# Weights converted in pieces of 1024 columns, and token blocks in another order, in a retention and two-MLP kernel

## The chip, the cores and the metric

The kernel runs on one core of one Trainium2 chip. Its time is the device time of one execution in microseconds; three runs of the kernel before took 897.42 to 898.11 us, with a median of 897.6 us.

## The reference

Attention with a decay in place of a softmax (retention), then two MLPs with the same shapes:

```python
scores = q @ k.T / sqrt(64)            # batch 4, heads 8, seq 576, head_dim 64
x = (scores * Dmat) @ v                # Dmat[i, j] = gamma_h ** (i - j) for i >= j, else 0
x = x.transpose(0, 2, 1, 3).reshape(2304, 512)
h = x @ moe_w_in                       # 512 x 2048
x = (h * sigmoid(h)) @ moe_w_out       # 2048 x 512
r = maximum(x @ moe2_w_in, 0)
out = (r * r) @ moe2_w_out             # 2304 x 512, float32
```

The weights come as float64, the rest as float32.

## The kernel before

**The products.** Each float32 operand is split into a high and a low part (`xh`, `xl`, `wh`, `wl`, `gh`, `gl`), and each product is three matmuls: high by high, high by low, low by high (`mm3`, L74). The 2304 tokens are cut into five blocks (`BLOCKS`), and `d_ff` into 16 columns of 128 (`f`). `seq` lists the steps (layer, block, f). A step runs `gemm1` (12 matmuls, 4 of 128 rows by 3) into the PSUM tile `ph`, and `gemm2` of the step two earlier (`LAG`) into `acc`. Between the two stands `gate`: the activation on ScalarE (L380 or L383), the product on VectorE (L381 or L384, `sg`), the copy `gh` on ScalarE (L388) and the rest `gl` on VectorE (L389). `later` and `flush` put these off by half a step each, so that on every engine they stand behind what was emitted before them. Engines run their queues in order.

**The weights.** All 64 wide weight tiles don't fit at once beside the rest: a layer's 16 `wh` and 16 `wl` tiles take the 32 buffers of pool `wp`, and each passes from layer 0 to layer 1 when its last matmul is done. The float64 words are turned into float32 by bit operations, in pieces of 512 columns (`w_in` and `w_out` of an `f` are one piece each): `load_w` fetches a raw piece on SyncE's queue, `conv_a` makes two ScalarE passes (L101, L102), `conv_b` a shift, an add and a sign operation on VectorE (L107 to L109), `conv_c` copies `wh` on ScalarE (L121), `conv_d` makes `wl` on VectorE (L125). Raw pieces have three buffers (`RAW`), and the load of a piece is issued when `conv_b` of the piece three before it is done. `conv_to` says how far the conversion has got: in the start-up by the table `ST_C`, in the first block of layer 0 two pieces a step, in the last block of layer 0 and the first of layer 1 nine eighths of a piece a step.

**The attention.** Eighteen units of 128 tokens, each a score product `P` (`scores`), a state of the past that GpSimd decays (`dS`, L290) and VectorE adds to (`S`, L284 and L286), a value product `Q` (`values`), and `whole`, which puts the two halves together and splits the result into `xh` and `xl`. The four units of the first block run ahead of the first step (the start-up); those of block j + 1 are spread over the steps of block j.

**Between the layers.** Layer 0 writes its result to DRAM (`x2`). `load_x2` fetches a block back on SyncE's queue into `xr`, and four copies on ScalarE (L442, `xh`) and four differences on VectorE (L443, `xl`) follow at once on their queues. It is called at step 8 of the last block of layer 0 and at step 4 of each block of layer 1.

Of the kernel before, what the change touches and what calls it, by code (L numbers as in the profile page):

```python
# [38 lines left out]
def kernel(  # L39
# [21 lines left out]
    xp = ctx.enter_context(tc.tile_pool(name="xp", bufs=2))  # L61
# [17 lines left out]
    order = sorted(range(2 * KF), key=lambda i: (i // 2 + i % 2 * LAG, i % 2))

    def w_at(n):

        layer, i = divmod(n, 2 * KF)
        return (layer, *divmod(order[i], 2))

    def load_w(n):
        layer, f, part = w_at(n)
        if n < W1_FIRST:
            r = wp.tile([128, 512], U64, tag="w", name="wr")
        else:  # L90
            r = rp.tile([128, 512], U64, tag="wr", name="wr")
        nc.sync.dma_start(out=r, in_=(w1, w2)[layer][f, part])  # L92
        raw_w[n] = r

    conv = {}

    def conv_a(n):
        r = raw_w.pop(n).bitcast(I32).rearrange("p (n t) -> p n t", t=2)
        lo, hi = r[:, :, 0], r[:, :, 1]
        t = rp.tile([128, 512], I32, tag="wt", name="t", bufs=3)  # L100
# [12 lines left out]
    def w_part(n):  # L113
        layer, f, part = w_at(n)
        if (layer, f) not in wt:
            wt[layer, f] = tuple(wp.tile([128, 1024], F32R, tag="w", name=nm) for nm in ("wh", "wl"))
        return (w[:, part * 512 : part * 512 + 512] for w in wt[layer, f])

    def conv_c(n):
        wh, _ = w_part(n)  # L120
        nc.scalar.copy(wh, conv[n][0].bitcast(F32))  # L121

    def conv_d(n):
        wh, wl = w_part(n)
        nc.vector.tensor_sub(wl, conv.pop(n)[0].bitcast(F32), wh)  # L125
# [12 lines left out]
    load_end = [2 * KF]  # L138
# [7 lines left out]
    def conv_to(layer, n):  # L146

        for i in range(conv_n[layer], min(n, 2 * KF + 2)):
            conv_n[layer] += 1
            for lag, stage in ((2, conv_c), (0, conv_a), (1, conv_b), (2, conv_d)):  # L150
                if 0 <= i - lag < 2 * KF:
                    stage(layer * 2 * KF + i - lag)
                    if stage is conv_b and n_loaded[0] < i - lag + layer * 2 * KF + RAW + 1:
                        load_next()
# [6 lines left out]
    x_t = {}  # L161
    block_of = []
# [7 lines left out]
    dS = [None]  # L170
# [73 lines left out]
    def scores(u, startup):  # L244
# [11 lines left out]
        rf = ap.tile([128, 2, 4, L], F32, tag="rf", name="rf", bufs=2)  # L256
# [8 lines left out]

        def first_state():
# [5 lines left out]
    def new_state(u, b, P):  # L272
# [9 lines left out]
        add = P[:, b, 256:512].rearrange("p (a d) -> p a d", a=4)  # L282
        if n == 0:
            nc.vector.tensor_copy(new, add)  # L284
        else:
            nc.vector.tensor_add(new, add, dS[0])  # L286
# [106 lines left out]
    def gemm2(layer, j, f):  # L393
# [6 lines left out]
        for t in range(nt):  # L400
# [10 lines left out]
            if f == KF - 1:  # L411
# [23 lines left out]
    def load_x2(j):  # L435
# [3 lines left out]
        xh = xp.tile([128, KD, NBMAX], F32R, tag="xh", name="xh")[:, :, 0:n]  # L439
        xl = xp.tile([128, KD, NBMAX], F32R, tag="xl", name="xl")[:, :, 0:n]  # L440
# [31 lines left out]
    while n_loaded[0] < W1_FIRST:  # L472
        load_next()
# [112 lines left out]
```

## Time and profile before

| | |
|---|---|
| median of three runs | 897.6 us (897.42 to 898.11) |
| profiled execution | 897.14 us |
| its span | 895.4 us |
| TensorE matmul busy | 862.8 us (96%) |
| VectorE busy | 427.6 us (48%) |
| ScalarE busy | 327.1 us (37%) |
| GpSimd busy | 72.8 us (8%) |

The span is the time from the first to the last instruction; the rest of the execution lies around it. PE is TensorE, PEld its weight loads, DVE VectorE, ACT ScalarE, POOL GpSimd, SPq and ACTq the instructions that issue DMAs on SyncE's and ScalarE's queues. A busy time is a share of the whole span, while the stages have different limits, so the rows below are by stretch. An arrow in brackets names what ended the idle time before an instruction.

### The profile page before, as it was taken

The numbers are of one execution on the slowest core, as the hardware profiler recorded it, in microseconds if no ns is written. First come the engines' busy times: TensorE is split into PE (matmuls) and PEld (weight loads), VectorE is DVE, ScalarE is ACT, GpSimd is POOL, SyncE is SP. The second block draws the span as 40 slices with busy tenths as digits, with TensorE's granted clock in tenths as the row PEclk, the third lists the DMA queues.
The fourth block names the chain that finished last, engine by engine and source line by source line (L and its number), as shares of the span: only waits on it lengthen the run. The fifth ranks groups of instructions, "written<-read, shape, count | busy, mean of one in ns | idle before, by whom it ended". The sixth has DMA issues, their size and how long they took to land.

```text
span 895.4 us, 14028 instructions
## 1 busy us (share of the span) xinstructions
PE 862.8 (96%) x5930; PEld 739.8 (83%) x5930; DVE 427.6 (48%) x722; ACT 327.1 (37%) x594; POOL 72.8 (8%) x105
## 2 busy tenths in 40 slices
PE   6698979999999999999999989999999999999998
PEld 5576758999999888888878878889999888888886
DVE  3899995333443333335767776632242233223222
ACT  3576663222222322225556555432232223222221
POOL 5210111111122021100000000000000000000000
PEclk8699999999999999999999999999999999999999
DMA  9445532111211213002343433020020020001001
GB/s 355 175 140 191 181 127 95 48 48 48 84 49 48 84 48 118 1 1 95 120 139 118 142 131 115 2 83 1 1 83 1 0 83 1 1 0 48 1 1 47
DMA packets 21662, 68.27 MB, mean 76 GB/s; under 512 B 2400, under 2 KB 4192, under 8 KB 21216
## 3 DMA queue, kind: packets, MB, share of 16 engines
q1 hardware_dynamic: 17280, 59.91, 19.5%
q10 hardware_dynamic: 4320, 7.47, 2.3%
q8 instruction: 46, 0.75, 0.3%
q14 instruction: 16, 0.13, 0.0%
HBM read 57.93 MB, written 9.44 MB: 75 GB/s over the span
## 4 chain that ended last, share of the span: by engine, by line
PE 82%; DVE 2%; DMA 1%; issue 0%; ACT 0%; SPq 0%; ACTq 0%
PE acc L74 40%; PE ph L74 39%; PE Q L301 2%; DMA xr<-x 1%; PE P L250 1%; PE P L255 1%; DVE xl L443 0%; DVE t L108 0%; DVE gl L389 0%; DVE t L109 0%; DVE t L107 0%; DVE wl L125 0%; PE Q L317 0%; ACT xh L442 0%; SPq L92 0%
## 5 line engine op out<-in xcount | busy, mean ns | idle before, releaser
L74 PE MATMUL ph<-xh,wh 128*128 128x512 f32 (+1 forms) x640 | 238.1, 372 | 5.6 <-ACT xh L335 5.6
L74 PE MATMUL ph<-xl,wh 128*128 128x512 f32 (+1 forms) x640 | 236.4, 369 | 0.0
L74 PE MATMUL ph<-xh,wl 128*128 128x512 f32 (+1 forms) x640 | 236.3, 369 | 0.0
L384 DVE SCALAR_TENSOR_TENSOR sg<-ph,sg 128x512 f32<-128x512 f32 (+1 forms) x80 | 51.0, 638 | 195.3 <-ACT sg L383 195.3
L74 PEld LDWEIGHTS ph<-xh,wh 128*128 128x128 f32 x640 | 120.8, 189 | 24.0 <-ACT xh L335 5.8
L74 PEld LDWEIGHTS ph<-xl,wh 128*128 128x128 f32 x640 | 120.7, 189 | 16.8 <-DVE xl L336 0.4
L74 PEld LDWEIGHTS ph<-xh,wl 128*128 128x128 f32 x640 | 120.7, 189 | 15.2
L74 PE MATMUL acc<-gl,wh 128*128 128x512 f32 (+1 forms) x320 | 120.2, 376 | 9.6 <-DVE gl L389 9.4
L389 DVE TENSOR_TENSOR gl<-sg,gh 128x512 fp32r<-128x512 f32 (+1 forms) x160 | 103.5, 647 | 52.9 <-ACT gh L388 52.6
L388 ACT CAST gh<-sg 128x512 fp32r<-128x512 f32 (+1 forms) x160 | 92.3, 577 | 91.2 <-DVE sg L384 51.5
L381 DVE TENSOR_TENSOR sg<-ph,sg 128x512 f32<-128x512 f32 (+1 forms) x80 | 50.9, 636 | 148.7 <-ACT sg L380 148.7
L74 PE MATMUL acc<-gh,wh 128*128 128x512 f32 (+1 forms) x320 | 120.5, 377 | 0.0
L383 ACT ACTIVATE sg<-ph 128x512 f32<-128x512 f32 (+1 forms) x80 | 44.5, 556 | 207.9 <-PE ph L74 207.5
L74 PE MATMUL acc<-gh,wl 128*128 128x512 f32 (+1 forms) x320 | 119.0, 372 | 0.0
L74 PE MATMUL acc<-wh,gl 128*128 128x512 f32 x288 | 112.8, 392 | 2.8 <-DVE gl L389 2.8
L74 PE MATMUL acc<-wl,gh 128*128 128x512 f32 x288 | 112.6, 391 | 0.0
L74 PE MATMUL acc<-wh,gh 128*128 128x512 f32 x288 | 112.0, 389 | 0.0
L380 ACT ACTIVATE sg<-ph 128x512 f32<-128x512 f32 (+1 forms) x80 | 44.3, 554 | 159.0 <-PE ph L74 159.0
L74 PEld LDWEIGHTS acc<-gl,wh 128*128 128x128 f32 x320 | 60.8, 190 | 21.3 <-DVE gl L389 13.9
L74 PEld LDWEIGHTS acc<-gh,wh 128*128 128x128 f32 x320 | 60.6, 189 | 8.7
L74 PEld LDWEIGHTS acc<-gh,wl 128*128 128x128 f32 x320 | 60.9, 190 | 7.4
L74 PEld LDWEIGHTS acc<-wh,gl 128*128 128x128 f32 x288 | 54.1, 188 | 14.6 <-DVE gl L389 3.2
(50 smaller groups left out, 738.0 us busy)
## 6 DMA issues: line engine op xcount, KB each, us to landing
wr<-w SPq DMA_DIRECT2D x64, 512.0 KB, 3.5
raw<-att SPq DMA_DIRECT2D x34, 512.0 KB, 5.3
x<-y ACTq DMA_DIRECT2D x12, 256.0 KB, 2.5
xr<-x SPq DMA_DIRECT2D x3, 1024.0 KB, 5.5
out<-y SPq DMA_DIRECT2D x10, 256.0 KB, 2.1
out<-y ACTq DMA_DIRECT2D x7, 256.0 KB, 2.3
x<-y ACTq DMA_DIRECT2D x8, 192.0 KB, 1.9
xr<-x SPq DMA_DIRECT2D x2, 768.0 KB, 5.3
```

Source lines behind the costliest of these rows:

```text
L74: mm(o, a, b, start=first and i == 0, stop=last and i == n - 1)
L250: mm(o, dims(u, a, e, b, 768), dims(u, a, e, b, 0), start=True, stop=True)
L255: mm(o, toks(u, a, e, b, 256), toks(u, a, e, b, 512), start=True, stop=True)
L301: mm(w, a, b, start=e not in started, stop=last)
L380: nc.scalar.activation(s, ph, ACTF.Sigmoid)
L381: nc.vector.tensor_mul(s, ph, s)
L383: nc.scalar.activation(s, ph, ACTF.Relu)
L384: nc.vector.scalar_tensor_tensor(s, ph, 0.0, s, op0=ALU.max, op1=ALU.mult)
L388: nc.scalar.copy(gh, s)
L389: later.append(lambda: nc.vector.tensor_sub(gl, s, gh))
```

## The change

`w_in` and `w_out` of an `f` become one piece of 1024 columns, except for the first three `f` of layer 0, which stay in two pieces of 512 (all three `w_in` first). Raw pieces have two buffers of twice the size. The three operations of `conv_b` are cut in two parts, and the parts of three neighbouring pieces are interleaved by half steps: `conv_to` counts half pieces. `ST_C` and `ST_F` say how many in the start-up and in the first steps, then two a step; for layer 1 it is 0.8 pieces a step in the last block of layer 0 and half a piece a step in layer 1. The blocks are 512, 384, 512, 384, 512 tokens, layer 1 takes them in the order 1, 0, 3, 2, 4, and the tiles of x have one buffer for even and one for odd blocks. The decayed state is written in place by GpSimd ahead of VectorE's sum, in the start-up one flush later.

```diff
-BLOCKS = [512, 384, 384, 512, 512]
+BLOCKS = [512, 384, 512, 384, 512]
-W1_FIRST, W1_AHEAD = 6, 5
+W1_FIRST = 3
-ST_C = (0, 0, 1, 2, 2, 3, 3, 4, 4)
-W2_LAG, W2_NUM, W2_DEN = 0, 9, 8
+ST_C = (0, 0, 2, 3, 4, 5, 5, 6, 7)
+ST_F = (7, 11, 15, 18)
+W2_LAG = 1
-RAW = 3
+RAW = 2
...
+    pieces = (
+        [(0, f, part, 1) for part in range(2) for f in range(W1_FIRST)]
+        + [(0, f, 0, 2) for f in range(W1_FIRST, KF)]
+        + [(1, f, 0, 2) for f in range(KF)]
+    )
...
+            r = rp.tile([128, 2, 512], U64, tag="wr", name="wr")
+        w = (w1, w2)[layer][f, part : part + m].rearrange("a p c -> p a c")
+        nc.sync.dma_start(out=r, in_=w)
...
+    def conv_raw(n):
+        lo, hi = words(n)
+        bits[n] = t = rp.tile([128, 1024], I32, tag="wt", name="t", bufs=2)[:, 0 : 512 * pieces[n][3]]
         nc.scalar.activation(t.bitcast(F32), hi.bitcast(F32), ACTF.Abs, scale=2.0**-112)
         nc.scalar.activation(lo, lo.bitcast(U32), ACTF.Copy, scale=2.0**-29)
+    def conv_add(n):
+        t = bits[n]
         nc.vector.tensor_scalar(t, t, 3, None, op0=ALU.logical_shift_left)
+        nc.vector.tensor_tensor(t, t, words(n)[0], op=ALU.add)
+    def conv_sign(n):
+        t, hi = bits[n], words(n)[1]
         nc.vector.scalar_tensor_tensor(
             t, hi, -(2**31), t, op0=ALU.bitwise_and, op1=ALU.bitwise_or
         )
+        raw_w.pop(n)
+        if n_loaded[0] <= n + RAW:
+            load_next()
...
     def conv_to(layer, n):
-        for i in range(conv_n[layer], min(n, 2 * KF + 2)):
+        last = n_pieces[layer]
+        for i in range(conv_n[layer], min(n, 2 * last + 3)):
             conv_n[layer] += 1
...
+            k, odd = divmod(i, 2)
+            todo = ((0, conv_raw), (1, conv_sign), (1, conv_wh)) if odd else ((1, conv_add), (2, conv_wl))
+            for lag, stage in todo:
+                if 0 <= k - lag < last:
+                    stage(layer * n_pieces[0] + k - lag)
...
+    def new_x(j):
+        return tuple(
+            xp.tile([128, KD, BLOCKS[j % 2]], F32R, tag=f"{nm}{j % 2}", name=nm) for nm in ("xh", "xl")
+        )
+    J2 = (1, 0, 3, 2, 4)
...
         def first_state():
             new_state(u, 0, P)
-            later.append(lambda: new_state(u, 1, P))
-        later.append(first_state)
+            decayed_state(u, 1)
+            later.append(second_state)
...
+        later.append((lambda: later.append(first_state)) if startup else first_state)
...
             if layer == 0 and j == 0:
-                conv_to(0, 2 * f + half + 1 + W1_AHEAD)
-            elif i > w2_base + W2_LAG:
-                conv_to(1, (2 * (i - w2_base - W2_LAG) + half - 1) * W2_NUM // (2 * W2_DEN))
+                n0, n1 = (ST_F[x] if x < len(ST_F) else ST_F[-1] + 2 * (x - len(ST_F) + 1) for x in (f, f + 1))
+                conv_to(0, n1 if half else (n0 + n1 + 1) // 2)
+            elif i >= w2_base + W2_LAG:
+                h = 2 * (i - w2_base - W2_LAG) + half + 1
+                conv_to(1, 4 * min(h, 2 * KF) // 5 + max(h - 2 * KF, 0) // 2)
...
             if layer == 0 and j == nb - 1 and f == KF - 8:
-                load_x2(0)
-            if layer == 1 and f == 4 and j + 1 < nb:
-                load_x2(j + 1)
+                load_x2(J2[0])
+            if layer == 1 and f == 4 and j != J2[-1]:
+                load_x2(J2[J2.index(j) + 1])
```

VectorE in the first block, from the gate product of step 1 (`sg`) to that of step 2, before (`t` is a piece under conversion, the number behind a name tells tiles apart; `wl_605` is that of step 3):

```order
L381 TENSOR_TENSOR sg_599<-ph_575,sg_599 128x512
L107 TENSOR_SCALAR t_589<-t_589 128x512
L108 ISA t_589<-wr_152,t_589 128x1024
L109 SCALAR_TENSOR_TENSOR t_589<-wr_152,t_589 128x512
L125 TENSOR_TENSOR wl_605<-t_567,wh_604 128x512
L107 TENSOR_SCALAR t_607<-t_607 128x512
L108 ISA t_607<-wr_154,t_607 128x1024
L109 SCALAR_TENSOR_TENSOR t_607<-wr_154,t_607 128x512
L125 TENSOR_TENSOR wl_542<-t_589,wh_541 128x512
L389 TENSOR_TENSOR gl_601<-sg_599,gh_600 128x512
L381 TENSOR_TENSOR sg_641<-ph_617,sg_641 128x512
```

The same stretch after the change (`wl_608` is that of step 3):

```order
L418 TENSOR_TENSOR sg_574<-ph_552,sg_574 128x512
L123 SCALAR_TENSOR_TENSOR t_565<-wr_140,t_565 128x512
L118 TENSOR_SCALAR t_579<-t_579 128x1024
L119 ISA t_579<-wr_150,t_579 128x2048
L136 TENSOR_TENSOR wl_533<-t_565,wh_532 128x512
L123 SCALAR_TENSOR_TENSOR t_579<-wr_150,t_579 128x1024
L118 TENSOR_SCALAR t_601<-t_601 128x1024
L119 ISA t_601<-wr_152,t_601 128x2048
L136 TENSOR_TENSOR wl_608<-t_579,wh_607 128x1024
L426 TENSOR_TENSOR gl_576<-sg_574,gh_575 128x512
L418 TENSOR_TENSOR sg_614<-ph_588,sg_614 128x512
```

Between the same two products there were two narrow pieces, and step 3's `wl` was the fourth operation behind the first product; now it is the eighth, with two wide shifts and adds and a wide sign ahead of it.

ScalarE in the first block, in the steps that follow, before (`wr` is a raw piece; L101 and L102 read it first):

```order
L102 ACTIVATE wr_686<-wr_686 128x512
L388 CAST gh_735<-sg_734 128x512
L121 CAST wh_604<-t_720 128x512
L101 ACTIVATE t_778<-wr_726 128x512
L102 ACTIVATE wr_726<-wr_726 128x512
L380 ACTIVATE sg_788<-ph_764 128x512
L121 CAST wh_793<-t_742 128x512
L101 ACTIVATE t_796<-wr_748 128x512
L102 ACTIVATE wr_748<-wr_748 128x512
L388 CAST gh_789<-sg_788 128x512
```

And after the change (L113 and L114 read it first, L417 is the sigmoid, L425 the copy `gh`):

```order
L417 ACTIVATE sg_695<-ph_677 128x512
L113 ACTIVATE t_700<-wr_654 128x1024
L114 ACTIVATE wr_654<-wr_654 128x1024
L132 CAST wh_706<-t_650 128x1024
L425 CAST gh_696<-sg_695 128x512
L417 ACTIVATE sg_739<-ph_722 128x512
L113 ACTIVATE t_744<-wr_704 128x1024
L114 ACTIVATE wr_704<-wr_704 128x1024
L132 CAST wh_750<-t_700 128x1024
```

Before, a step's two pieces stood apart, one on each side of the sigmoid; now one wide piece stands between a step's sigmoid and its `gh`, and the next sigmoid is behind both.

SyncE's queue at the first reload of x (`xr`), before:

```order
L92 DMA wr_4410<-w2 128x512
L92 DMA wr_4452<-w2 128x512
L92 DMA wr_4470<-w2 128x512
L438 DMA xr_4486<-x2_0_85 128x2048
L92 DMA wr_4524<-w2 128x512
L92 DMA wr_4568<-w2 128x512
```

After the change:

```order
L96 DMA wr_4226<-w2 128x2x512
L96 DMA wr_4270<-w2 128x2x512
L475 DMA xr_4294<-x2_1_86 128x1536
L96 DMA wr_4332<-w2 128x2x512
L96 DMA wr_4376<-w2 128x2x512
```

The reload stands behind a raw piece in both, before behind one of 512 columns, now behind one of 1024; the block that is fetched is now that of 384 tokens.

## Rows read from the trace of the kernel before

**Rows 1.** Engines by stretch: start:end, length, busy us of PE, PEld, DVE, ACT, POOL, clock, DMA
```profile
35.23:50.81 15.58, 15.17 (x96) 11.65 (x97) 14.40 (x24) 11.30 (x20) 1.97 (x2) 0.84 0.11 35
50.81:138.14 87.33, 77.90 (x594) 60.24 (x592) 82.10 (x137) 57.99 (x101) 13.03 (x15) 0.98 0.50 164
140.00:430.00 290.00, 290.00 (x2644) 261.11 (x2643) 112.92 (x200) 82.37 (x155) 40.00 (x58) 1.00 0.17 59
436.00:462.00 26.00, 24.13 (x100) 19.48 (x99) 16.14 (x28) 13.57 (x25) 0.00 (x0) 0.93 0.38 122
```

**Rows 2.** What TensorE waited for: us in total, times, longest us
```profile
PE acc L74 <- DVE gl L389: 12.2, 10, 2.8
```

**Rows 3.** VectorE in order of time, start-up: start us, us, line, operation [idle before]
```profile
16.28 0.42 DVE L286 TENSOR_TENSOR S<-P,dS 128x256 f32<-128x256 f32 x1 [2.42 <-POOL dS L290]
...
29.01 0.98 DVE L109 SCALAR_TENSOR_TENSOR t<-wr,t 128x512 int32<-128x512 int32 x1
```

**Rows 4.** VectorE in order of time, first token block
```profile
41.43 0.69 DVE L381 TENSOR_TENSOR sg<-ph,sg 128x512 f32<-128x512 f32 x1 [0.66 <-ACT sg L380]
42.04 0.42 DVE L107 TENSOR_SCALAR t<-t 128x512 int32<-128x512 int32 x1
42.49 0.69 DVE L108 CUSTOM_DVE_ANT_0 t<-wr,t 128x1024 uint16<-128x1024 uint16 x1
43.21 0.69 DVE L109 SCALAR_TENSOR_TENSOR t<-wr,t 128x512 int32<-128x512 int32 x1
43.82 0.69 DVE L125 TENSOR_TENSOR wl<-t,wh 128x512 fp32r<-128x512 f32 x1
44.43 0.42 DVE L107 TENSOR_SCALAR t<-t 128x512 int32<-128x512 int32 x1
...
46.90 1.22 DVE L389 TENSOR_TENSOR gl<-sg,gh 128x512 fp32r<-128x512 f32 x1
```

**Rows 5.** TensorE in order of time, first matmul of steps 0, 3 and 15, and a stall
```profile
35.23 0.80 PE L74 MATMUL ph<-xh,wh 128*128 128x512 f32 x1 [5.58 <-ACT xh L335]
...
50.81 0.39 PE L74 MATMUL ph<-xh,wh 128*128 128x512 f32 x1
...
83.86 0.50 PE L74 MATMUL acc<-gl,wh 128*128 128x512 f32 x1 [2.38 <-DVE gl L389]
...
85.06 0.63 PE L74 MATMUL acc<-gh,wl 128*128 128x512 f32 x1
...
138.14 0.39 PE L74 MATMUL ph<-xh,wh 128*128 128x512 f32 x1
```

**Rows 6.** Groups by line and shape: count | busy us, mean ns | idle
```profile
L101 ACT ACTIVATE t<-wr 128x512 f32<-128x512 f32 x64 | 43.2, 675 | 12.0 <-DMA wr<-w 9.3 <-DVE gl L389 1.7 <-DVE wl L125 1.0
...
L380 ACT ACTIVATE sg<-ph 128x512 f32<-128x512 f32 x48 | 28.6, 595 | 81.1 <-PE ph L74 81.1
...
L380 ACT ACTIVATE sg<-ph 128x384 f32<-128x384 f32 x32 | 15.7, 492 | 77.8 <-PE ph L74 77.8
...
L443 DVE TENSOR_TENSOR xl<-xr,xh 128x512 fp32r<-128x512 f32 x12 | 7.5, 687 | 8.4 <-ACT xh L442 8.4
...
L443 DVE TENSOR_TENSOR xl<-xr,xh 128x384 fp32r<-128x384 f32 x8 | 3.9, 554 | 6.3 <-ACT xh L442 6.3
```

**Rows 7.** DMA issues: count, KB each, median us from issue to landing
```profile
wr<-w SPq DMA_DIRECT2D x64, 512.0 KB, 3.5
...
xr<-x SPq DMA_DIRECT2D x3, 1024.0 KB, 5.5
```

**Rows 8.** First reload of x: SyncE, ScalarE and TensorE in order of time
```profile
446.92 0.38 SPq L438 DMA_DIRECT2D xr<-x  x1
...
452.44 2.18 ACT L442 CAST xh<-xr 128x512 fp32r<-128x512 f32 x4 [6.38 <-DMA xr<-x]
...
456.24 0.50 PE L74 MATMUL acc<-gl,wh 128*128 128x512 f32 x1 [1.87 <-DVE gl L389]
```

**Rows 9.** Second reload of x: TensorE in order of time
```profile
526.48 0.50 PE L74 MATMUL acc<-wh,gl 128*128 128x512 f32 x1 [2.83 <-DVE gl L389]
```

More of the change, by code (lines that the diff above doesn't have):

```diff
@@ L78 @@
     raw_w = {}
[L79 to L84, printed above, removed]
+    bits = {}
+    pieces = (
[3 more added lines that the diff above has]
+    )
+    n_pieces = (len(pieces) - KF, KF)
     def load_w(n):
-        layer, f, part = w_at(n)
-        if n < W1_FIRST:
-            r = wp.tile([128, 512], U64, tag="w", name="wr")
-        else:
-            r = rp.tile([128, 512], U64, tag="wr", name="wr")
-        nc.sync.dma_start(out=r, in_=(w1, w2)[layer][f, part])
+        layer, f, part, m = pieces[n]
+        if m == 1:
+            r = wp.tile([128, 1, 512], U64, tag="w", name="wr")
+        else:
+            r = rp.tile([128, 2, 512], U64, tag="wr", name="wr")
+        w = (w1, w2)[layer][f, part : part + m].rearrange("a p c -> p a c")
+        nc.sync.dma_start(out=r, in_=w)
@@ L93, in load_w, with words, parts @@
         raw_w[n] = r
[L95 to L100, printed above, removed]
+    def words(n):
+        r = raw_w[n].bitcast(I32).rearrange("p a (n t) -> p (a n) t", t=2)
+        return r[:, :, 0], r[:, :, 1]
+    def parts(n):
+        layer, f, part, m = pieces[n]
+        if (layer, f) not in wt:
+            wt[layer, f] = tuple(wp.tile([128, 1024], F32R, tag="w", name=nm) for nm in ("wh", "wl"))
+        return (w[:, part * 512 : (part + m) * 512] for w in wt[layer, f])
@@ L111, in conv_b, with conv_wh, conv_wl @@
         )
[L113 to L125, printed above, removed]
+        raw_w.pop(n)
+        if n_loaded[0] <= n + RAW:
+            load_next()
+    def conv_wh(n):
+        wh, _ = parts(n)
+        nc.scalar.copy(wh, bits[n].bitcast(F32))
+    def conv_wl(n):
+        wh, wl = parts(n)
+        nc.vector.tensor_sub(wl, bits.pop(n).bitcast(F32), wh)
     later = []
@@ L281, in new_state @@
             new = ap.tile([128, 4, D], F32, tag="S", name="S", bufs=3)
[L282 to L286, printed above, removed]
-        S_at[i + 1] = new
-        if n + 1 < PER - 1:
-            dS[0] = ap.tile([128, 4, D], F32, tag="dS", name="dS", bufs=1)
-            nc.gpsimd.tensor_mul(dS[0], new, dec.unsqueeze(2).to_broadcast([128, 4, D]))
+        if n:
+            nc.gpsimd.tensor_mul(new, S_at[i], dec.unsqueeze(2).to_broadcast([128, 4, D]))
+        S_at[i + 1] = new
+    def new_state(u, b, P):
+        n = place(u, b)
+        if n < PER - 1:
+            new = S_at[2 * u + b + 1]
+            add = P[:, b, 256:512].rearrange("p (a d) -> p a d", a=4)
+            if n == 0:
+                nc.vector.tensor_copy(new, add)
+            else:
+                nc.vector.tensor_add(new, add, new)
     def values(u, startup):
@@ L321, in values @@
         if j not in x_t:
-            x_t[j] = tuple(
-                xp.tile([128, KD, NBMAX], F32R, tag=nm, name=nm) for nm in ("xh", "xl")
-            )
+            x_t[j] = new_x(j)
         xh, xl = (x[:, :, t0 : t0 + C] for x in x_t[j])
@@ L438, in load_x2 @@
         nc.sync.dma_start(out=r, in_=x2[j])
-        xh = xp.tile([128, KD, NBMAX], F32R, tag="xh", name="xh")[:, :, 0:n]
-        xl = xp.tile([128, KD, NBMAX], F32R, tag="xl", name="xl")[:, :, 0:n]
+        if j == J2[-1]:
+            xh, xl = (rp.tile([128, KD, n], F32R, tag="wr", name=nm) for nm in ("xh", "xl"))
+        else:
+            xh, xl = new_x(j)
         for k in range(KD):
@@ L500 @@
     ps_o = ctx.enter_context(tc.tile_pool(name="ps_o", bufs=4, space=bass.MemoryType.PSUM))
-    seq = [(layer, j, f) for layer in range(2) for j in range(nb) for f in range(KF)]
+    seq = [(layer, j, f) for layer in range(2) for j in (range(nb), J2)[layer] for f in range(KF)]
     w2_base = (nb - 1) * KF
@@ L521 @@
                 ap_ctx.close()
-                load_end[0] = 4 * KF
+                load_end[0] = len(pieces)
                 for _ in range(RAW):
```

38 lines of the change are left out of this document (19 added, 19 removed).

## The prediction

> **What bounds the kernel now.** I read the busy time by stretch first. Between 140 and 430 us TensorE is busy for all of 290 us at full clock [rows 1]: there only matmuls count, and the change leaves their number and sizes as they are (three blocks of 512 tokens and two of 384 in either order). So the time can change only where TensorE is not full: before 35.23 us, in the first token block (35.23 to 138.14 us) and at the two reloads of x (436 to 462 and 502 to 535 us). The table of waits says who ends most of these gaps: VectorE's `gl`, 12.2 us in ten waits [rows 2]. In the first block VectorE is busy for 82.1 of 87.33 us (TensorE for 77.9): there VectorE, which converts the weights, sets the pace [rows 1].
>
> The rows of VectorE give the pace from start to start: shift 0.45, add 0.72, sign 0.61, `wl` 0.61 us, so one piece of 512 columns takes 2.39 us, a gate product 0.61 us [rows 4]. Twelve steps of the first block, from step 3 (50.81 us) to step 15 (138.14 us) [rows 5], hold two pieces, a product and a `gl` each: 12 x (2 x 2.39 + 2 x 0.61) = 72.0 us. The other 15.3 of the 87.3 us are attention, VectorE slowed beside GpSimd (the `gl` at 46.90 us took 1.22 us where other operations of its size take 0.69 [rows 4]) and short waits: 1.28 us a step.
>
> **The change part by part**, against the profiled execution: 897.14 us, a span of 895.4 us and 1.74 us around it. The median of the runs is 897.6 us, 0.5 above, and I add the sum to that.
>
> *Start-up: -2.1 us.* VectorE is the engine behind from 16.28 us on, and what is left on its queue ahead of the last `xl` sets the first matmul at 35.23 us [rows 3, 5]. Two things go: one sign operation (0.98 us beside GpSimd, at 29.01 us) now stands behind the last `xl`, and a shift and an add (1.2 us) stand ahead of the state sum that waited 2.42 us for GpSimd [rows 3]. Late next is the same chain of states through GpSimd. Bounds: -3.4 (all of the 2.42 us and 0.98) to +0.5 (the first state is now copied after the second score product, and a value product waits for it).
>
> *Step 3 of the first block: +4.7 us.* A wide operation costs a fixed part once: 512 against 384 columns took 687 against 554 ns on VectorE, so 512 columns more are +0.53 us, and 595 against 492 ns on ScalarE, so +0.41 us [rows 6]. The shift has no second size: with the same fixed part of 155 ns (687 less 4 x 133) its 420 ns become 690. That it doubles, or adds nothing, changes the sum by 0.3 us a step at most. So wide: shift 0.72, add 1.25, sign 1.14, `wl` 1.14, a piece 4.25 us where two narrow ones were 4.78 us. But the order is worse at the beginning: the product of step 0 starts 6.2 us after the first matmul (41.43 less 35.23) and VectorE can't pass it, since before it only one shift and add, one sign and one `wl` are left to do. Behind it, up to the `wl` of step 3, now stand three narrow signs (1.83), two narrow shifts and adds (2.34), three narrow `wl` (1.83), two products and a `gl` (1.83), two wide shifts and adds (3.94), a wide sign and a wide `wl` (2.28): 14.05 us. With 0.55 us of GpSimd's slowing that `wl` is ready 20.8 us after the first matmul. Two matmuls of step 3 can go ahead of it, so step 3 starts some 20.3 us after step 0, before 15.6 us [rows 5]. Bounds 3 and 6.
>
> *The clock after that wait: +0.9 us.* TensorE idles some 5 us there. After the 5.58 us before the first matmul, and after 2.38 us at 83.86 us, matmuls took 0.63 to 0.80 us where 0.39 is usual, at half clock, 1.2 of 2.4 GHz; the stretch has 0.84 of the full clock [rows 1, 5]. Eight such matmuls are 1.9 us, but steps 4 and 5 wait for VectorE as well, so I take half. Bounds 0 and 1.9.
>
> *Steps 3 to 15: -0.3 us.* VectorE alone would need 4.25 + 1.22 + 1.28 = 6.75 us a step, 81.0 us for twelve, 6.3 us less than before. What speaks against it is the ring of raw tiles, two where there were three. The load of a piece is issued when the sign of the piece two before it is done, and the piece comes up two steps later. One turn: sign 1.14, issue 0.15, landing, two ScalarE passes 2.1 (675 ns and 0.41, the second overlapping 0.1), shift and add 1.97, `wl` of the piece before 1.14, `gl` and product 1.22, then the next sign but one. Landing: a 512 KB load takes 3.5 us, the 1,024 KB reload of x 5.5 us [rows 7]. I take 5.5, the row of the same size. A turn is then 13.2 us, with one step's attention 14.5 us for two steps: six turns are 87.0 us, before 87.3. Bounds: 81.0 (VectorE decides) to 93 (landing 6.5, when two 512 KB loads of attention stand in the same queue). In this sum ScalarE, idle a third of the stretch [rows 1], waits for DMA with the sigmoid queued behind that wait: TensorE then waits for it through product and `gl`.
>
> The Trainium skill, page "SBUF — State Buffer", section "The DMA setup-cost knee", gives about 2 us fixed and 436 GB/s: 3.2 us for 512 KB, 4.4 us for 1 MiB. The first agrees with the row (3.5); by the second a turn is 13.4 us and the twelve steps some 81 us, and the change is a gain: the first rival below.
>
> *First reload of x: +0.8 us.* The load of x stood behind a weight load that waits for a sign, was issued at 446.92 us, and ScalarE stood 6.38 us in the copies; TensorE waited 1.87 us, and the stretch ran at 0.93 of the clock, 1.8 us more over 26 us: 3.7 us [rows 1, 8]. Now the sign stands ahead of the step's product, so x is issued earlier, and the first block is 768 KB and not 1,024 KB; but a load of 1 MB stands before it, and in the next step a wide add and `wl` (3.1 us) stand ahead of the late `gl`. These about cancel (2 to 3 us of wait); behind it ScalarE's wait for the next ring load delays two more `gl` by under 1 us each. I take 4.5 us; bounds 2 and 7.
>
> *Second reload: -2.1 us.* It cost 2.83 us [rows 9]. Now only half a piece is converted a step there, the load waits for a sign of the step before, and no conversion stands ahead of the `gl`; but steps of 384 tokens leave less room. I count 0.7 us of wait; bounds 0 and 2.8.
>
> *Costed at nothing:* the attention's state product, now in place and behind the query products on GpSimd, which is 14% to 15% busy there [rows 1]; if its cover is gone, 0.6 us a unit in the first block. The tiles of x by parity and the order 1, 0, 3, 2, 4 keep each reload a block ahead of its use. Fewer issues on SyncE.
>
> Sum: -2.1 + 4.7 + 0.9 - 0.3 + 0.8 - 2.1 = +1.9 us: 899.0 us against the profiled run, 899.5 us on the scale of the median.
>
> **Rivals.**
> 1. *Faster: the ring closes.* If 1 MB lands in 4.7 us or less, a turn with attention is 13.7 us or less, and VectorE's 6.75 us a step decides: steps 3 to 15 take 81 to 82 us, -5.7, and the wait at step 3 is paid back. For it: the 512 KB row at 3.5 us and the reload's 5.5, which shared its queue; VectorE's 94% in the stretch [rows 1, 7]. Against: the only loads of that size here have a median of 5.5 us. -2.1 + 4.7 + 0 - 5.7 + 0.8 - 2.1 = -4.4: 893.2 us. From a landing of 4.9 us down (six turns of 0.6 us less) the sum lies 1.7 us or more below before.
> 2. *Clearly slower: ScalarE's wait spreads.* With 6.2 us of landing a turn is 15.2 us (+3.9 us), step 3's half clock is paid in full (1.9), and at the first reload the chain sign, load, ScalarE, `gl` loses 2.5 us: -2.1 + 4.7 + 1.9 + 3.9 + 2.5 - 2.1 = +8.8: 906.4 us. For it: VectorE's `gl` already ends ten waits [rows 2].
> 3. *Nothing to measure:* step 3's wait is given back by what VectorE saves later, and the two reloads cancel: 897.6 us.
>
> **How the numbers follow.** The forecast has 0.44 (its own range 896.5 to 903), rival 1 0.28, rival 2 0.14, rival 3 0.14. Within 0.2%, 1.8 us, a measurement of this kernel can't tell a change from none. Of the forecast's 0.44, 0.17 lie within that and 0.02 below. Faster: 0.28 + 0.02 + 0.01 = 0.31; same: 0.17 + 0.12 = 0.29; slower: 0.25 + 0.14 + 0.01 = 0.40. The range from 890.5 (rival 1 with a further 2.7 us, when the start-up or the first reload gain their bounds) to 905.5 us leaves out the upper part of rival 2.
>
> **What would show it.** Right: a wait of TensorE of 4 to 6 us ahead of step 3, some 20 us after the first matmul; ScalarE waiting for DMA 1 us or more in most steps of the first block; the first matmul at 33 us; a shorter wait in the second reload. Wrong: no DMA waits of ScalarE in the first block and step 15 before 134 us (rival 1), or a new wait outside these stretches, where I count nothing.

## The result, and the profile after

The changed kernel takes 905.99 us (median of four runs, 905.68 to 906.14), the kernel before on the same chip 897.86 us: a ratio of 1.0089, 95% interval 1.0072 to 1.0107. The profiled execution has a span of 904.4 us, 9.0 more than before. So the change costs 8.1 us where 1.9 were forecast, and the time lies just above the range.

The starts of the steps show where. The times are those of the first matmul of a step (steps counted through both layers; 144 is the first of the last block of layer 1), in us:

| stretch | before | after | difference | forecast |
|---|---|---|---|---|
| start to step 0 | 35.23 | 33.81 | -1.4 | -2.1 |
| step 0 to 3 | 15.58 | 21.04 | +5.5 | +4.7 |
| step 3 to 15 | 87.33 | 83.49 | -3.8 | -0.3, and +0.9 for the clock |
| step 15 to 144 | 660.72 | 669.62 | +8.9 | -1.3 (two reloads) |
| step 144 to the end | 96.5 | 96.4 | -0.1 | 0 |

The first block, on which most of the working was spent, comes out even: its waits and its gains cancel to +0.2 us at step 15. What is measured lies behind it, in steps 74 to 87, where the second layer's weights are converted and two blocks of x reloaded.

Engines by stretch of the kernel after, with the columns of [rows 1] and in the same order (the first block's two parts from its own step starts):

```profile
33.81:54.85 21.04, 15.54 (x96) 11.60 (x96) 16.11 (x23) 13.33 (x20) 4.24 (x4) 0.82 0.06 10
54.85:138.34 83.49, 78.14 (x593) 61.94 (x593) 75.76 (x90) 50.82 (x65) 15.70 (x12) 0.95 0.47 170
140.00:430.00 290.00, 290.00 (x2643) 260.97 (x2642) 112.38 (x192) 82.22 (x147) 40.59 (x59) 1.00 0.17 61
436.00:462.00 26.00, 21.43 (x90) 17.36 (x89) 17.77 (x23) 13.78 (x18) 0.00 (x0) 0.95 0.30 112
```

Between 140 and 430 us TensorE is full, as before. From step 3 to 15 VectorE fell from 94% to 91% busy. Around the first reload TensorE lost 2.7 us of busy time.

What TensorE waited for after, us in total, times, longest (before: [rows 2]):

```profile
PE acc L75 <- DVE gl L426: 9.2, 7, 4.6
PE ph L75 <- ACT wh L132: 5.2, 2, 4.9
PE ph L75 <- DVE wl L136: 5.1, 4, 1.8
PE ph L75 <- ACT xh L372: 4.5, 1, 4.5
```

TensorE in order of time, the first matmul of steps 0 and 3 [rows 5], the first reload [rows 8] and the second reload [rows 9]:

```profile
33.81 0.80 PE L75 MATMUL ph<-xh,wh 128*128 128x512 f32 x1 [4.49 <-ACT xh L372]
...
54.85 0.80 PE L75 MATMUL ph<-xh,wh 128*128 128x512 f32 x1 [4.91 <-ACT wh L132]
...
459.43 0.80 PE L75 MATMUL acc<-gl,wh 128*128 128x512 f32 x1 [4.57 <-DVE gl L426]
460.03 0.63 PE L75 MATMUL acc<-gh,wl 128*128 128x512 f32 x1
...
527.31 0.66 PE L75 MATMUL acc<-wh,gl 128*128 128x512 f32 x1 [2.94 <-DVE gl L426]
```

The waits for `gl` come to 9.2 us, less than before's 12.2, and yet the kernel is slower. Not in that sum are the wait of 4.91 us at step 3, and the matmuls of 0.63 us behind the long waits, at 1.2 of 2.4 GHz. Step 74 took 11.79 us instead of 5.44: 4.57 of wait and 1.8 at half clock.

ScalarE and SyncE around the first reload, in order of time (before: [rows 8]):

```profile
438.01 1.15 ACT L113 ACTIVATE t<-wr 128x1024 f32<-128x1024 f32 x1 [2.42 <-DVE wl L136]
439.07 1.13 ACT L114 ACTIVATE wr<-wr 128x1024 int32<-128x1024 uint32 x1
440.08 1.04 ACT L132 CAST wh<-t 128x1024 fp32r<-128x1024 f32 x1
441.02 0.60 ACT L417 ACTIVATE sg<-ph 128x512 f32<-128x512 f32 x1
...
445.42 1.15 ACT L113 ACTIVATE t<-wr 128x1024 f32<-128x1024 f32 x1 [2.42 <-DVE wl L136]
...
448.43 0.58 ACT L417 ACTIVATE sg<-ph 128x512 f32<-128x512 f32 x1
...
453.27 1.75 ACT L481 CAST xh<-xr 128x384 fp32r<-128x384 f32 x4 [2.88 <-DMA xr<-x]
```
```profile
447.09 0.34 SPq L475 DMA_DIRECT2D xr<-x  x1
```

VectorE between the two raw passes:

```profile
441.65 0.69 DVE L418 TENSOR_TENSOR sg<-ph,sg 128x512 f32<-128x512 f32 x1 [1.99 <-ACT sg L417]
442.26 0.68 DVE L118 TENSOR_SCALAR t<-t 128x1024 int32<-128x1024 int32 x1
442.98 1.22 DVE L119 CUSTOM_DVE_ANT_0 t<-wr,t 128x2048 uint16<-128x2048 uint16 x1
444.12 1.22 DVE L136 TENSOR_TENSOR wl<-t,wh 128x1024 fp32r<-128x1024 f32 x1
```

From one raw pass to the next, and from one `sg` to the next, are 7.41 us, where a step of TensorE has 5.44. The rows give this turn operation by operation, from start to start: two raw passes 1.06 and 1.01, `wh` 0.94, the sigmoid 0.63, its product on VectorE 0.61, shift 0.72, add 1.14, `wl` 1.30. The next raw pass waits 2.42 us for that `wl`: it belongs to the piece two before, whose `t` buffer the pass needs, and there are only two. So in a step with a piece, four in five here, the gates fall 2 us behind. The sigmoid of step 69 starts 0.1 us after the last matmul that it reads, those of steps 70, 71 and 72 start 0.6, 2.7 and 4.7 us after theirs; the reload meets a gate that is late already. Behind the copies, VectorE:

```profile
453.82 1.96 DVE L482 TENSOR_TENSOR xl<-xr,xh 128x384 fp32r<-128x384 f32 x4 [4.08 <-ACT xh L481]
455.70 0.69 DVE L118 TENSOR_SCALAR t<-t 128x1024 int32<-128x1024 int32 x1
456.42 1.23 DVE L119 CUSTOM_DVE_ANT_0 t<-wr,t 128x2048 uint16<-128x2048 uint16 x1
457.56 1.22 DVE L136 TENSOR_TENSOR wl<-t,wh 128x1024 fp32r<-128x1024 f32 x1
458.69 0.68 DVE L426 TENSOR_TENSOR gl<-sg,gh 128x512 fp32r<-128x512 f32 x1
```

Its `gl` at 458.69 us, that of step 72, is what TensorE waited for, and 3.0 us of conversion stand between it and the last `xl`.

### The profile page after: what moved, and what is told of

Same layout as the page of the kernel before. It is cut to its first block, busy times and chain, and to the rows that moved or that the text cites. A ratio compares the mean times of both kernels' runs of the same rounds, so it can differ in the third digit from the quotient of the medians.

```text
span 904.4 us, 13757 instructions
## 1 busy us (share of the span) xinstructions
PE 865.6 (96%) x5930; PEld 741.1 (82%) x5930; DVE 411.3 (45%) x606; ACT 316.2 (35%) x507; POOL 77.7 (9%) x105
## 4 chain that ended last, share of the span: by engine, by line
PE 73%; DVE 5%; ACT 4%; DMA 3%; issue 2%; ACTq 0%; SPq 0%; DVEq 0%
PE acc L75 35%; PE ph L75 35%; PE Q L340 2%; DMA wr<-w 2%; DMA xr<-x 1%; DVE wl L136 1%; DVE t L119 1%; ACT t L113 1%; PE P L272 1%; ACT wh L132 1%; ACT wr L114 1%; DVE t L118 1%; DVE t L123 1%; PE P L277 1%; DVE xl L482 0%
## 5 line engine op out<-in xcount | busy, mean ns | idle before, releaser
L75 PEld LDWEIGHTS ph<-xh,wl 128*128 128x128 f32 x640 | 121.5, 190 | 22.5 <-DVE wl L136 7.1
L425 ACT CAST gh<-sg 128x512 fp32r<-128x512 f32 (+1 forms) x160 | 92.4, 578 | 92.7 <-DVE sg L421 54.1
L417 ACT ACTIVATE sg<-ph 128x512 f32<-128x512 f32 (+1 forms) x80 | 44.4, 555 | 146.8 <-PE ph L75 146.8
```

Of the source, the lines that this page charges most:

```text
L75: mm(o, a, b, start=first and i == 0, stop=last and i == n - 1)
L417: nc.scalar.activation(s, ph, ACTF.Sigmoid)
L425: nc.scalar.copy(gh, s)
```

## The experiments

The theory, A: wide conversion in the second layer, which stands ahead of the gates on ScalarE and VectorE, makes them late, and the two reloads, which stop ScalarE for a landing, find no slack. Each text on record says what its rival is. The columns give the median of 4 to 10 executions, its ratio to before, and the length of three stretches in us. The stretches come from one execution of each kernel; those of e2 (902.58 us) and f4 (892.21) lay 2.0 and 1.2 us below their medians, that of g3 (904.18) 2.2 above.

| kernel | median | ratio (95%) | to step 0 | 0 to 15 | 15 to 144 |
|---|---|---|---|---|---|
| before | 897.9 to 898.1 | 1 | 35.2 | 102.9 | 660.7 |
| changed | 905.99 | 1.0089 (1.0072, 1.0107) | 33.8 | 104.5 | 669.6 |
| e1 gate first | 909.47 | 1.0133 (1.0115, 1.0151) | 33.7 | 104.9 | 672.2 |
| e2 three t | 904.59 | 1.0069 (1.0052, 1.0085) | 33.0 | 104.0 | 667.4 |
| e3 reload apart | 897.41 | 0.9994 (0.9985, 1.0004) | 33.6 | 105.4 | 660.6 |
| e4 fill step 0 | 905.70 | 1.0080 (1.0063, 1.0096) | 33.8 | 103.7 | 669.9 |
| e5 order alone | 900.61 | 1.0025 (1.0016, 1.0035) | 35.9 | 102.3 | 663.5 |
| f1 before apart | 890.81 | 0.9913 (0.9895, 0.9930) | 36.0 | 103.0 | 653.8 |
| f3 order apart | 893.63 | 0.9948 (0.9928, 0.9968) | 35.2 | 102.4 | 656.6 |
| f4 all three | 893.42 | 0.9945 (0.9926, 0.9965) | 33.5 | 102.9 | 657.6 |
| g1 pace | 891.20 | 0.9932 (0.9913, 0.9951) | 34.1 | 104.1 | 654.7 |
| g3 pace alone | 902.02 | 1.0052 (1.0033, 1.0070) | 33.8 | 104.0 | 668.2 |
| g2 pace and all | 889.67 | 0.9914 (0.9891, 0.9938) | 33.4 | 103.1 | 654.4 |

**e1, the gates ahead of the conversion.** In the second layer's conversion:

```diff
             elif i >= w2_base + W2_LAG:
+                flush()
...
-            flush()
+            if i < w2_base + W2_LAG:
+                flush()
```

> From the second layer's conversion on, each half step emits the gate's operations ahead of the conversion's, nothing else changes. Theory A (the wide conversion stands ahead of the sigmoid on ScalarE and waits there for the difference two pieces back or for its load, so that the gates run about 5 us late and the two reloads of x find no slack): the sigmoid starts within 1 us of its product, TensorE's waits from 440 us on fall from some 11 us to under 5, time 4 to 8 us less than the changed kernel, 898 to 902 us. Rival B (the gates' place does not matter, the wide loads and the order of blocks delay the reloads themselves): waits of 4.6 and 2.9 us remain, time within 1.5 us of 906.

It was slower, by 2.5 us behind step 15. ScalarE's copies, VectorE's late `gl`, and the load of x, in this kernel:

```profile
456.03 1.75 ACT L481 CAST xh<-xr 128x384 fp32r<-128x384 f32 x4 [3.48 <-DMA xr<-x]
```
```profile
458.46 0.68 DVE L426 TENSOR_TENSOR gl<-sg,gh 128x512 fp32r<-128x512 f32 x1
```
```profile
449.89 0.34 SPq L475 DMA_DIRECT2D xr<-x  x1
```

No conversion stands between the last `xl` and this `gl` any more. But the sign now runs behind the gate's product, so the weight load ahead of x on SyncE, and x itself, go out 2.8 us later, and the `gl` is ready at the same time as before the edit (458.46 against 458.69 us). What is new is lost in steps 81 and 82 (4.5 us more than in the changed kernel). Both theories missed, A's 898 to 902 us and B's 1.5 us around 906. Nor did the gates come in time: the sigmoid of step 70 starts 4.0 us after its product, not within 1 us as expected, and raw passes still follow one another by 7.4 us in most of the stretch. So this edit doesn't tell what the place ahead of the gate costs; it tells that another place doesn't shorten the turn.

**e2, a third `t`.** Every third piece of the second layer gets a buffer of its own.

```diff
-        bits[n] = t = rp.tile([128, 1024], I32, tag="wt", name="t", bufs=2)[:, 0 : 512 * pieces[n][3]]
+        if n >= n_pieces[0] and n % 3 == 2:
+            t = late["pool"].tile([128, 1024], I32, tag="t3", name="t", bufs=1)
+        else:
+            t = rp.tile([128, 1024], I32, tag="wt", name="t", bufs=2)[:, 0 : 512 * pieces[n][3]]
+        bits[n] = t
```

> A third tile for the words under conversion in the second layer, order unchanged. If it is the wait for the difference two pieces back (16.8 us of ScalarE's idle time there) that holds the sigmoid, theory A by way of the buffers: ScalarE's waits for that difference vanish, time 3 to 6 us less, 900 to 903 us. If the order alone holds it (ScalarE then waits for the load or for the sign operation at the same place): under 1.5 us less.

It gave 1.4 us of 8, not the 3 to 6 of theory A. ScalarE's waits for the `wl` of the piece two before, 16.8 us behind 400 us, are gone, but others stand in their place, as the rival has it: for loads 13.5 us where it was 7.9, for the sign 15.4 where it was 3.4. TensorE's waits at the reloads stayed at 3.56 and 2.95 us.

**e3, the reloads apart from the conversion.**

```diff
-            if layer == 0 and j == nb - 1 and f == KF - 8:
+            if layer == 0 and j == nb - 1 and f == 1:
                 load_x2(J2[0])
-            if layer == 1 and f == 4 and j != J2[-1]:
+            if layer == 1 and f == (12 if j == J2[0] else 4) and j != J2[-1]:
```

> The two reloads of x that fall into the second layer's conversion are moved out of it: to step 1 of the last block of layer 0 and to step 12 of the first block of layer 1. Theories A and B both: the waits of 4.6 and 2.9 us and their half clock go, 6 to 9 us less, 897 to 900 us. A theory C (the conversion's own chain is too slow and the loss only moves) expects new waits of TensorE of 3 us or more in the same stretch and under 3 us less.

As expected: 8.6 us back, all of them behind step 15, which clears the first block. But 660.6 us is still 6.8 above the 653.8 of f1 (below), in which TensorE waits for nothing there. The rest is the 7.4 us turn, now alone. ScalarE in steps 77 and 78 of this kernel:

```profile
470.45 1.20 ACT L113 ACTIVATE t<-wr 128x1024 f32<-128x1024 f32 x1 [2.42 <-DVE wl L136]
...
473.45 0.64 ACT L417 ACTIVATE sg<-ph 128x512 f32<-128x512 f32 x1
...
477.90 1.23 ACT L113 ACTIVATE t<-wr 128x1024 f32<-128x1024 f32 x1 [2.42 <-DVE wl L136]
...
480.91 0.67 ACT L417 ACTIVATE sg<-ph 128x512 f32<-128x512 f32 x1
```

From sigmoid to sigmoid 7.46 us, with no reload near, and the lateness adds up: the sigmoids of steps 74 to 77 start 3.6, 4.7, 6.8 and 8.6 us after their products.

**e4, more conversion in step 0.** `ST_F` counts half pieces, so this moves conversion, not attention, in f4 and g2 too, whose texts on record call it attention.

```diff
-ST_F = (7, 11, 15, 18)
+ST_F = (9, 12, 15, 18)
```

> Two more half pieces are converted in step 0 of the first block, where VectorE stood idle for 3.45 us ahead of the first gate product; the steps after 2 are as they were. As forecast, that queue sets step 3: step 3 comes 1.5 to 2.5 us earlier after step 0 (21.0 us before), and TensorE's wait there falls from 4.9 to about 3 us. If the ring of raw tiles decides the rest of the block, step 15 is earlier by under 1 us and the time falls by under 1 us; if VectorE decides, by 1.5 to 2.5 us.

Step 3 came 1.1 us sooner after step 0 (19.90 us), less than the 1.5 to 2.5 expected, and the wait there fell from 4.91 to 4.47 us only; step 15 came sooner by 0.8. The median moved by 0.3, inside the runs' spread. One trace can't show so little, but there are nine with this first block: the six without the edit take 19.98 to 21.07 us from step 0 to 3 and 103.98 to 105.36 to step 15, the three with it (e4, f4, g2) 18.88 to 19.91 and 102.85 to 103.70. By their means the edit gives 1.3 us at either step, so what it saves at step 3 is not taken back by the ring.

**e5, f1 and f3: narrow conversion.** e5 is the kernel before with the new order of the blocks alone; f1 is the kernel before with the reloads moved as in e3; f3 has both.

```diff
-BLOCKS = [512, 384, 384, 512, 512]
+BLOCKS = [512, 384, 512, 384, 512]
...
+    J2 = (1, 0, 3, 2, 4)
...
-    seq = [(layer, j, f) for layer in range(2) for j in range(nb) for f in range(KF)]
+    seq = [(layer, j, f) for layer in range(2) for j in (range(nb), J2)[layer] for f in range(KF)]
```

> The kernel before, narrow conversion as it was, with only the blocks 512, 384, 512, 384, 512 and the second layer's order 1, 0, 3, 2, 4. Theory A (the wide conversion under the reloads loses the time): 897 to 900 us, waits at the two reloads of 2 to 4 us each as before. Rival C (the order of the blocks loses it: a block of 384 tokens first in the second layer has steps of 4.1 us for the same conversion): 903 to 906 us, with most of the loss between step 74 and the end of the second layer's first block.

> The kernel before, with only the two reloads moved: x of the second layer's first block is loaded in step 1 of the last block of layer 0 (was step KF - 8), and the next one in step 12 of the second layer's first block (was step 4). Theory A (a reload costs what it costs because it falls among the weights' conversion): the 1.9 us of wait, the 1.8 us of half clock at the first reload and the 2.83 us at the second go away, 898 - 6.5 = 891 to 893 us. Rival B (the change's own conversion in the second layer loses the time, a reload among narrow conversion costs nothing that moving gives back): 896 to 898 us, and then the changed kernel's 897.4 us with its reloads moved is no worse than before.

> Narrow conversion, the new order of blocks and the two reloads moved apart (step 1 of layer 0's last block; step 12 of the second layer's first block). Beside the changed kernel with the same reloads (897.4 us) this leaves only the wide conversion with its earlier stages different. Theory A: 891 to 894 us, so that the wide conversion by itself costs 3 to 6 us, the step 3 wait of 5.5 us above all. Rival C: the short steps have no room for the conversion, 896 us or more.

f1 came out just below theory A's figure: the two reloads cost the kernel before 6.9 us, and the rival of its text falls. e5 lies between A and C, with its loss where C put it. TensorE at its two reloads:

```profile
455.31 0.50 PE L74 MATMUL acc<-gl,wh 128*128 128x512 f32 x1 [0.61 <-DVE gl L390]
...
521.19 0.80 PE L74 MATMUL acc<-wh,gl 128*128 128x512 f32 x1 [6.80 <-DVE gl L390]
```

The first reload became cheaper than before (384 tokens to fetch and copy), the second dearer: 6.80 us where it was 2.83 [rows 9]. Two things make it so. The block fetched there is now that of 512 tokens and no longer one of 384: from the issue of x to the late `gl` pass 11.1 us where it was 9.8. And the steps around it have 384 tokens, 4.19 us each, so that the two steps between a `gl` and its use have 8.4 us and not 10.9. With the reloads moved the new order still costs 2.8 us: f3 (as A expected, but what it saves against e3 lies behind step 15, not at step 3) has one wait in the second layer, of 2.27 us at 548.61: the end of the narrow conversion still lies under a reload at step 12 of a short block.

Against f1's 653.8 us between steps 15 and 144:

| lost there, us | reloads as given | reloads apart |
|---|---|---|
| narrow, old order | 6.9 | 0 |
| narrow, new order | 9.7 | 2.8 |
| wide, new order | 15.8 | 6.8 |

As differences of this table, the change's 8.9 us are 2.8 for the order, 4.0 for the wide conversion, and 2.1 because the two meet at the reloads. As a split of causes this is rough. f3's 2.8 us are nearly all in step 94 (6.72 us for 4.19), where no kernel with wide conversion waits; g2 (below), in the new order too, loses 0.6 us in all, so the order by itself costs no more than that. And "wide" is also a quicker pace: the kernel before converts nine eighths of a narrow piece a step, which is 0.56 of a wide one, the change 0.8.

**f4, e2 to e4 together.** The three edits above, unchanged.

> The changed kernel with its reloads moved apart, a third t tile for the second layer's pieces, and step 0 of the first block filled with attention later (ST_F 9, 12, 15, 18). Theory A: with the reloads apart, t's second buffer holds up only short waits, so the sum of the two small edits counts: 897.4 - 1 to - 4 = 893 to 896.5 us. Rival: the third t tile gains only where a reload is late, so nothing is left of it: 896.5 to 898 us.

The median lies in theory A's range, so the rival falls. Behind step 15 its trace takes 657.6 us: the third `t` gives 3.0 of e3's 6.8 lost us (alone it gave 2.3 there), by single traces that both lay below their medians. 3.8 are left, and ScalarE waits 17.2 us for loads and 12.7 for signs behind 400 us; the waits for loads point to the two raw tiles as the next limit, but three of them were not tried.

**g1, g3 and g2: the pace.** 0.7 pieces a step where it was 0.8, in g1 with the reloads apart, in g3 alone, in g2 with all of f4. In g1 and g2 the second reload is at step 13, behind the last of the conversion, where e3 and f4 have 12.

```diff
-                conv_to(1, 4 * min(h, 2 * KF) // 5 + max(h - 2 * KF, 0) // 2)
+                conv_to(1, 7 * min(h, 30) // 10 + max(h - 30, 0) // 2)
```

> The changed kernel with the reloads moved apart (step 1 of layer 0's last block; step 13 of the second layer's first block) and the second layer's conversion paced at 0.7 pieces a step until step 80 (was 0.8). With the reloads apart and 0.8 the trace shows 6.5 us lost in steps 74 to 82, where the raw pass of a piece waits for the wl two pieces before it: a turn of that chain is 7.4 us, and at 0.8 a piece is asked for every 6.8 us, at 0.7 every 7.8. Theory A (the conversion falls behind because its turn is longer than its pace): most of it goes, 893 to 895.5 us. Rival D (each wide piece delays its own step's gate, whatever the pace): 896.5 to 898 us, as with 0.8.

> The changed kernel with only the pace of the second layer's conversion changed (0.7 for 0.8 until step 80); the reloads stay where the change has them. Theory A (two separate losses: late gates in steps 78 to 82 of 4.4 us, and the two reloads): the reloads' waits of 4.6 and 2.9 us stay, the other goes, 902 to 904 us. Rival E (the reload is what makes the conversion late, so pace alone gives nothing): 905 to 907 us.

> The same, with the third t tile in the second layer and attention later in the first block's step 0 (9, 12, 15, 18). At 0.8 these two edits gave 893.4 us, with 3.5 us still lost in steps 78 to 82. Theory A: 890 to 892 us, the second layer without a wait of 1 us but the y copy's. Rival D: 893 to 894 us.

g1: 6.8 lost us became 0.9, the time lies 1.8 us below theory A's range, and rival D falls. At 0.8 a piece is due every 6.8 us, at 0.7 every 7.8, and the turn of 7.4 us lies between: from step 69 on the sigmoids, up to 8.6 us late in e3, are at most 3.0 us late in g1, and 0.1 us in most steps. At 0.7 g1 still converts quicker than the narrow kernel (0.56), so at that pace width by itself costs under 1 us. Narrow pieces at the change's pace were not run.

g3 hit theory A's time, but not in theory A's way. The load of x at its first reload, ScalarE's copies, and the `gl` behind them:

```profile
441.66 0.34 SPq L475 DMA_DIRECT2D xr<-x  x1
```
```profile
450.34 1.75 ACT L481 CAST xh<-xr 128x384 fp32r<-128x384 f32 x4 [4.78 <-DMA xr<-x]
```
```profile
452.77 0.69 DVE L426 TENSOR_TENSOR gl<-sg,gh 128x512 fp32r<-128x512 f32 x1
```

ScalarE stood longer than in the changed kernel (4.78 against 2.88 us), and TensorE did not wait at all. Counted from the start of step 74, the `gl` starts 5.4 us sooner than in the changed kernel. Of these, 2.4 are the landing: the sign that lets the loads go comes sooner, and x is issued 9.6 us ahead of step 74 and not 4.7. The other 3.0 are the conversion that no longer stands between the last `xl` and the `gl`. What was saved there came back later; that a slower conversion runs longer under the second reload would explain it, but no run takes this apart. TensorE in steps 82 and 86:

```profile
499.65 0.77 PE L75 MATMUL acc<-wh,gh 128*128 128x512 f32 x1 [2.94 <-DVE y L468]
...
524.51 0.79 PE L75 MATMUL acc<-wh,gl 128*128 128x512 f32 x1 [4.61 <-DVE gl L426]
```

Of the 8.0 us gained from step 64 to 81 (91.2 us where the changed kernel took 99.2), 6.5 were lost again up to step 96, in this execution, the slowest of the five. The expectation had it the other way round: the waits at both reloads should have stayed.

g2 is the best of all: 889.67 us (888.78 to 890.43), a shade below theory A's range, without a wait of TensorE behind 400 us, and faster than the kernel before by 0.6 to 1.1% and than the changed one by 16 us. f1, narrow conversion with two numbers changed, reaches 890.81 (889.76 to 891.44); whether g2 beats that too, these runs don't tell.

## Why the prediction was wrong

**Start-up: right, -1.4 for -2.1.** The four traces with the old start-up have step 0 at 35.22 to 36.01 us, the nine with the new one at 33.03 to 34.11: by their means 2.0 us apart. The state sum still waits for GpSimd, 1.82 and 0.72 us where it was 2.42 [rows 3].

**Step 3: right in size, +5.5 for +4.7**, with the wait of 4 to 6 us that was named (4.91), and for the most part by the way that was named, VectorE's queue. Only the end differs: not VectorE's `wl` let step 3 go but ScalarE's `wh`, which stood behind the raw passes of the next piece, and these had waited for the second `t` buffer:

```profile
51.70 1.15 ACT L113 ACTIVATE t<-wr 128x1024 f32<-128x1024 f32 x1 [2.25 <-DVE wl L136]
...
53.77 1.03 ACT L132 CAST wh<-t 128x1024 fp32r<-128x1024 f32 x1
```

The sign that this `wh` needs was done at 52.81 us, so standing behind the raw passes cost 1.0 us. The `wl` of step 3 was ready at 56.27 us, 22.5 after the first matmul where 20.8 were worked out. The wide operations cost what the two sizes gave: start to start, shift 0.72, add 1.14 and `wl` 1.13 us in the rows of the first reload, and the sign 1.13, together 4.1 us a piece for 4.25. Over the whole kernel, mean ns of one:

```profile
L136 DVE TENSOR_TENSOR wl<-t,wh 128x1024 fp32r<-128x1024 f32 x29 | 36.7, 1265 | 1.1 <-ACT wh L132 1.1
L119 DVE CUSTOM_DVE_ANT_0 t<-wr,t 128x2048 uint16<-128x2048 uint16 x29 | 36.0, 1243 | 4.4 <-ACT wr L114 2.4 <-ACT gh L425 0.5
...
L123 DVE SCALAR_TENSOR_TENSOR t<-wr,t 128x1024 int32<-128x1024 int32 x29 | 35.2, 1214 | 0.0
L113 ACT ACTIVATE t<-wr 128x1024 f32<-128x1024 f32 x29 | 33.3, 1147 | 52.6 <-DMA wr<-w 26.4 <-DVE wl L136 19.4 <-issue 3.3
...
L118 DVE TENSOR_SCALAR t<-t 128x1024 int32<-128x1024 int32 x29 | 20.3, 700 | 1.5 <-ACT t L113 1.4
```

The last row but one shows what was overlooked: ScalarE's raw pass waited 26.4 us for loads, which was foreseen, and 19.4 us for `wl`, that is for the second `t` buffer, which stands in no term of the sum; 16.8 of them lie in the second layer.

**Steps 3 to 15 and the clock: -3.8 for +0.6.** The ring decided, as forecast (ScalarE waited eight times for a load there, 18.5 us in all), but a load landed sooner:

```profile
wr<-w SPq DMA_DIRECT2D x29, 1024.0 KB, 4.9
```

5.5 us, the reload's row [rows 7], was the wrong one to take, since that reload was issued 0.4 us behind a weight load in the same queue. By the forecast's own working, 0.6 us less of landing are 3.6 less in six turns: 83.4 us, measured 83.49. That it fits so closely is in part luck: the 83.4 hold nothing for the clock, whose +0.9 us can't be read apart (granted 0.95 in the stretch, 0.98 before). The Trainium skill's fit (page "SBUF — State Buffer", section "The DMA setup-cost knee"), by which 1 MiB is estimated at 4.4 us, was about as far off on the other side; the measurement lies between the two and decides.

**The first reload, +0.8: this step failed.** It was put that the earlier issue, the smaller block and the conversion ahead of the `gl` "about cancel". They didn't: counted from the start of step 74, the `gl` starts 2.7 us later than before. The conversion costs 3.0, as counted, and a slower landing 0.7; the smaller block gives back 0.6, and the earlier issue, on which the sum relied, 0.3 (x goes out 4.7 us ahead of step 74 where it was 4.4). Step 74 took 2.6 us more than before (11.79 against 9.19), still inside the bounds given. Outside them are steps 78 to 82, which lost 4.4 us more, where at most two delays of under 1 us were counted. The prediction took the gates and the signs for in time at the reload, and asked only what stands behind it. No term prices the conversion's own turn, 7.4 us, against the pace that the change asks of it, a piece every 6.8 us. e3 shows that this makes the gates late with no reload near (6.8 us), g1 that the pace decides it (0.9 us), and in g3 the same reload, met in time, costs nothing.

**The second reload, -2.1: this failed too.** "No conversion stands ahead of the `gl`", it said. SyncE, ScalarE and VectorE in order of time:

```profile
516.77 0.46 SPq L475 DMA_DIRECT2D xr<-x  x1
```
```profile
523.64 2.18 ACT L481 CAST xh<-xr 128x512 fp32r<-128x512 f32 x4 [4.21 <-DMA xr<-x]
```
```profile
520.65 1.22 DVE L136 TENSOR_TENSOR wl<-t,wh 128x1024 fp32r<-128x1024 f32 x1
...
524.29 2.50 DVE L482 TENSOR_TENSOR xl<-xr,xh 128x512 fp32r<-128x512 f32 x4 [2.42 <-ACT xh L481]
526.70 0.55 DVE L426 TENSOR_TENSOR gl<-sg,gh 128x384 fp32r<-128x384 f32 x1
```

An add and a `wl` do stand ahead of the four `xl`, but they cost nothing: VectorE stood idle for 2.42 us behind them. What the `gl` waited for is the reload itself. It now fetches 512 tokens in place of 384, which the prediction left out, and x landed 6.84 us after its issue, behind a weight load of 1,024 KB, where it took 4.93 before; the four `xl` take 2.50 us. Steps 86 and 87 lost 4.7 us, half clock included, where step 86 lost 3.1 before: +1.6, outside the bounds. That steps of 384 tokens "leave less room" was seen, and 0.7 us of wait counted; e5 shows the price of both, the larger block and the shorter steps: 6.80 us of wait with narrow conversion.

The two terms together: +8.6 for -1.3, and that is the miss. That the time lies only 0.5 us outside the range is luck: the first block came out 3.0 us better than forecast and hides part of it. The prediction's own sign of being wrong, a new wait outside its stretches, came with steps 78 to 82; of its signs of being right the last, a shorter wait at the second reload, did not (2.94 us for 2.83).

**Rival 2** came near with its time (906.4) and with 2.5 us at the first reload, but by luck: its 6.2 us of landing and its 3.9 us in the first block did not happen. **Rival 1** came half true: the landing was 4.9 us where it wanted 4.7, and steps 3 to 15 gained 3.8 of its 5.7 us; its two reloads are the forecast's and failed with them.

Left open: what the first block would gain without the ring. VectorE has 6.3 us less to do there from step 3 on (75.76 for 82.10), and 3.8 came out; three raw tiles of double size were not tried.

## What to carry to other kernels

A stage that runs on the side has a turn of its own, from buffer to buffer across engines: work it out and compare it with the pace at which the schedule asks for it, before pricing anything that meets it. Where the turn was the longer here (7.4 us for 6.8), the gates fell further behind with each piece, and the issue of a transfer that hung on the same chain fell behind with them. A slower pace alone gave 4.0 us back, a third buffer alone 1.4, moving the transfers out of the stretch 8.6. When blocks change places, look also at what each transfer now fetches and beside which steps it lands.

## What the runs showed of the hardware

A wait of TensorE can cost more than its length. 4.57 us at the first reload made the step 6.35 us longer, 6.80 us in e5 made it 8.5 longer: the matmuls behind them took 0.63 to 0.80 us, at 1.2 of 2.4 GHz, for some 1.7 us of time more. Not every wait does so, and not by its length alone: before, 1.87 us at the first reload were followed by such matmuls (the step was 3.75 us longer), while 2.83 us at the second were not (3.13 longer):

```profile
526.48 0.50 PE L74 MATMUL acc<-wh,gl 128*128 128x512 f32 x1 [2.83 <-DVE gl L389]
526.82 0.39 PE L74 MATMUL acc<-wh,gh 128*128 128x512 f32 x1
```

In the other direction, an engine may stand for long at no cost: ScalarE's 6.5 us at g3's first reload (4.78 of wait, 1.75 of copies) moved no matmul.
